# Top-k attention and SwiGLU on one Trainium2 core: units by query tile, FFN blocks across batches, and an issue order written out by hand

## The chip, the cores and the metric

The kernel runs on one core of one Trainium2 chip. The metric is the device time of an execution in microseconds (us). The engines are named as in the profile: PE is TensorE (PEld its weight loads), DVE is VectorE, ACT is ScalarE, POOL is GpSimd, and SP issues DMAs.

## The reference

There are 8 batches of 8 heads with 576 tokens and head dimension 64. For each head the scores are `q k^T / 8`; in each row only scores that are at least the row's 32nd largest are kept; softmax over those; product with `v`. The heads side by side give `x` of 4608 x 512. Then the feed-forward network (FFN):

```python
g = x @ w_gate                              # 512 x 1536
silu = g * (1.0 / (1.0 + np.exp(-g)))
val = x @ w_val                             # 512 x 1536
return (silu * val @ w_out).astype(np.float32)   # 1536 x 512
```

The weights arrive as float64. The kernel computes in float32.

## The kernel before

A pair of heads fills 128 partitions. The 576 tokens of a head are four tiles of 128 and a last one of 64. A unit of attention is (pair of heads, tile of queries), all five tiles of one pair before the next pair: 32 pairs, 160 units. In a full unit each head has its own tile of 128 queries; in the last unit of a pair the 64 queries of both heads share one.

The functions, with lines of the profile:
- `load` (L145) issues 12 DMAs for K, Q and V of a pair on SP (L152, L155). `prep` (L158) transposes K and Q on PE, copies them to SBUF on ACT, and puts V beside a column of ones on POOL (L184, L185).
- `scores` (L195): per head two products (512 and 64 keys) with contraction 64 (L206), then a copy to SBUF on ACT (L211).
- `select` (L214): four rounds of the eight largest (L227) with three of replacement between them (L237), on DVE. After the first, POOL makes the bias (L229) and ACT the exponentials (L231). At the end DVE multiplies the exponentials by the mask `s >= 32nd largest` (L240, two tensors read).
- `turn` (L250): ten transposes on PE (L260, L266) and three copies on ACT (L261, L267).
- `values` (L275): ten products in which the turned weights are the stationary operand and V with its ones (65 columns) the moving one (L287). The last column is the row's sum; DVE makes its reciprocal (L295, L296), ACT scales (L299), PE transposes to the layout of `x` transposed (L303), ACT copies (L306).
- `feed` (L316): the FFN of a batch in three blocks of 192 tokens. Twelve gate products (L326, four matmuls each) are copied to SBUF (L336), ACT takes a sigmoid of all at once (L338), POOL multiplies once over 2304 columns (L339), then twelve value products, each multiplied in from PSUM by DVE (L341), and the output products (L348), for a tile of 128 tokens and one of 64 with 512 columns each.
- `weights` and `rounded` (L127, L87): 72 pieces of 128 x 256 float64 weights are loaded by DMAs on POOL's queue (L91) and rounded on DVE, POOL and ACT.

A float32 matmul appears in the trace as two passes, and a transpose as one.

The order of the work comes from the loop at L368, which issues for each unit the next scores, its selection, the turn of the unit before, four pieces of FFN or weights, and the values of two units before; a scheduler then reorders instructions on every engine by their readiness as it estimates it. The FFN of a batch can start once the batch's attention is done. `ps_t` has two buffers for all transposes and value products.

Of the kernel before, what the change touches and what calls it, by code (L numbers as in the profile page):

```python
# [14 lines left out]
P = 128  # L15
TOP_K = 32
LOWEST = -3.4028234663852886e38
EPS = 1.0e-9
BLK = 192
WP = 256  # L20
HUGE = 122880.0  # 1151 << 20 as a float32's bits
LEAST = 3.4332275390625e-05  # 897 << 20 as a float32's bits
# [3 lines left out]
def kernel(  # L26
# [10 lines left out]
    """Top-k attention, then SwiGLU, in float32 throughout.  # L37

    Attention goes by unit (batch, pair of heads, tile of queries): the scores
    of both heads, the 32nd largest of each row by four rounds of max and three  # L40
    of match_replace, exp(s - max) zeroed below it, and the product with the
    values, whose last column of ones gives the sum of the row. A pair of heads
    is one 128-row slab of x transposed, which is what the first products of
    the FFN want. The FFN of a batch runs between the units of the next one.

    The tokens of a head are laid out as 4 tiles of the tokens 4 p + j, j < 4,
    and a last one of 64, so that each partition reads 1 KiB in one piece.

    The weights come in float64 and are rounded to float32 here, on their bits,
    while the first batch's attention runs.  # L50
    """
# [9 lines left out]
    DE = D + 1  # L61
    scale = 1.0 / float(D) ** 0.5
    assert D == 64 and R == 64 and H * D == DM and DM == 512 and S % BLK == 0

    consts = ctx.enter_context(tc.tile_pool(name="consts", bufs=1))
    ld = ctx.enter_context(tc.tile_pool(name="ld", bufs=2))
    work = ctx.enter_context(tc.tile_pool(name="work", bufs=2))
    small = ctx.enter_context(tc.tile_pool(name="small", bufs=4))
    conv = ctx.enter_context(tc.tile_pool(name="conv", bufs=2))
    ffn = ctx.enter_context(tc.tile_pool(name="ffn", bufs=2))  # L70
    ps_s = ctx.enter_context(tc.tile_pool(name="ps_s", bufs=2, space=PSUM))
    ps_t = ctx.enter_context(tc.tile_pool(name="ps_t", bufs=2, space=PSUM))
    ps_f = ctx.enter_context(tc.tile_pool(name="ps_f", bufs=2, space=PSUM))
# [3 lines left out]
    NV = 3  # L77
    vbufs = []
    for i in range(NV):
        vt = consts.tile([P, 2, J + 1, DE], FP32, name=f"v{i}")  # L80
        nc.gpsimd.memset(vt[:], 1.0)
        vbufs.append(vt)
# [4 lines left out]
    def rounded(src, dst):  # L87
# [36 lines left out]
            op0=ALU.is_ge, op1=ALU.mult,  # L124
        )

    def weights():  # L127
        pieces = []
        for src, dst in ((w_gate, wg), (w_val, wv), (w_out, wo)):
            for c in range(dst.shape[1]):  # L130
# [291 lines left out]
```

## Time and profile before

| what | value |
|---|---|
| median of three runs | 2607.87 us (2604.3, 2607.87, 2608.07) |
| span of the profiled execution, first to last instruction | 2599.7 us |
| median minus that span | 8.2 us |
| mean granted PE clock | 0.976 |
| busy 0 to 100 us: PE, DVE | 58, 79 us |
| busy 300 to 400 us: PE, DVE | 71, 94 us |
| busy 1100 to 1400 us: PE, DVE, ACT, POOL | 284, 236, 127, 25 us |
| busy 2430 to 2600 us: PE, DVE | 148, 12 us |
| matmul passes, DVE, ACT, POOL instructions | 12160, 4136, 2108, 473 |

The profiled execution's own time is that of its span; the runs' times include what lies before its first and after its last instruction. Engines work side by side, so their busy times are not to be added: at each stage the engine without idle time sets the pace, and idle time of the others costs nothing. A group line gives the line of the code, engine, operation, `out<-in`, shapes, count, then busy us, mean ns of one, idle us before it and what ended that wait. A timeline line gives the start, the time covered, and in brackets the idle time before it.

### The profile page before, as it was taken

To read this page: it belongs to the slowest core of one execution; us is meant where nothing else is said; L and a number is where in the kernel's file an instruction comes from. 1 tells how busy PE (TensorE), PEld (TensorE's weight loads), DVE (VectorE), ACT (ScalarE), POOL (GpSimd) and SP (SyncE) were. 2 spreads that over 40 slices of the span, in tenths; PEclk is the share of its full clock that TensorE was granted. 3 is DMA by queue.
4 is the path that set the end of the run, shared out by engine and by line. 5 is a ranking of instruction groups with operands and counts; after the bars stand their busy time and mean duration, and the time that the engine had idled before them with its cause. 6 is when DMAs were issued, how large, how long until landed. Compare 5 with 4: busy or idle time off the path is not lost. (4 is left out here: it accounts for less than half of the span.)

```text
span 2599.7 us, 33003 instructions
## 1 busy us (share of the span) xinstructions
PE 2325.9 (89%) x12160; PEld 1733.6 (67%) x12160; DVE 1911.0 (74%) x4136; ACT 971.4 (37%) x2108; POOL 314.3 (12%) x473
## 2 busy tenths in 40 slices
PE   5656579999999999999999999999999999999898
PEld 3444456667767668668667668668668667677666
DVE  7889898778787788769777788769768788765000
ACT  3333234335334335334434434434425434423111
POOL 3434321011011011011001001001101101000000
PEclk9999998999999999999999999999999999999999
DMA  3222110000000000000000000000000000000000
GB/s 100 61 67 71 62 34 14 21 17 19 21 19 17 20 7 19 16 21 15 21 20 15 21 16 19 7 20 15 21 20 15 21 16 1 7 7 5 7 5 11
DMA packets 128032, 58.75 MB, mean 23 GB/s; under 512 B 118656, under 2 KB 118656, under 8 KB 127872
## 3 DMA queue, kind: packets, MB, share of 16 engines
q1 hardware_dynamic: 122112, 37.78, 6.0%
q0 software_dynamic: 5760, 18.88, 2.4%
q8 instruction: 96, 1.57, 0.3%
q14 instruction: 64, 0.52, 0.1%
HBM read 47.19 MB, written 9.44 MB: 22 GB/s over the span
## 5 line engine op out<-in xcount | busy, mean ns | idle before, releaser
L227 DVE MAX8 m<-rest 128x8 f32<-128x576 f32 x864 | 619.8, 748 | 1.7
L326 PE MATMUL f<-xT,wv 128*128 128x192 f32 x2304 | 459.3, 349 | 76.1 <-DVE h L341 75.9
L348 PE MATMUL f<-wo,h 128*128 128x512 f32 (+1 forms) x1152 | 506.6, 595 | 0.0
L326 PEld LDWEIGHTS f<-xT,wv 128*128 128x128 f32 x2304 | 400.0, 203 | 99.0 <-DVE h L341 85.0
L287 PE MATMUL av<-v,et 128*128 128x65 f32 (+3 forms) x3200 | 455.4, 287 | 3.2 <-ACT et L261 3.0
L287 PEld LDWEIGHTS av<-v,et 128*128 128x128 f32 (+3 forms) x3200 | 417.4, 195 | 58.1 <-issue 14.1
L326 PE MATMUL f<-xT,wg 128*128 128x192 f32 x2304 | 419.6, 331 | 6.5 <-ACT g L336 6.5
L237 DVE MATCH_REPLACE8 rest<-m,rest 128x576 f32<-128x576 f32 x576 | 424.5, 742 | 0.0
L326 PEld LDWEIGHTS f<-xT,wg 128*128 128x128 f32 x2304 | 370.8, 191 | 22.1 <-ACT g L336 10.7
L348 PEld LDWEIGHTS f<-wo,h 128*128 128x128 f32 (+1 forms) x1152 | 183.0, 163 | 291.2 <-issue 288.1
L206 PE MATMUL s<-kT,qT 64*128 64x64 f32 (+3 forms) x1280 | 297.9, 483 | 84.3 <-ACT sc L211 84.1
L211 ACT COPY sc<-s 128x576 f32<-128x576 f32 x288 | 182.1, 642 | 438.1 <-PE s L206 323.4
L295 DVE TENSOR_SCALAR rinv<-av 128x2 f32<-128x2 f32 (+1 forms) x160 | 25.0, 156 | 358.2 <-PE av L287 351.2
L206 PEld LDWEIGHTS s<-kT,qT 64*128 64x128 f32 (+1 forms) x1280 | 154.2, 193 | 184.3 <-ACT sc L211 88.8
L231 ACT ACTIVATE e<-sc,bias 128x576 f32<-128x576 f32 x288 | 213.3, 771 | 166.8 <-POOL bias L229 166.3
L240 DVE SCALAR_TENSOR_TENSOR e<-sc,m,e 128x576 f32<-128x576 f32 x288 | 273.2, 981 | 2.0
L341 DVE TENSOR_TENSOR h<-h,f 128x192 f32<-128x192 f32 x288 | 96.9, 348 | 227.3 <-POOL h L339 134.6
L227 DVE MAX8 m<-sc 128x8 f32<-128x576 f32 x288 | 212.4, 749 | 35.3 <-ACT sc L211 33.9
L229 POOL TENSOR_SCALAR bias<-m 128x2 f32<-128x2 f32 (+1 forms) x160 | 34.8, 217 | 1480.2 <-DVE m L227 1344.1
L237 DVE MATCH_REPLACE8 rest<-m,sc 128x576 f32<-128x576 f32 x288 | 212.8, 742 | 0.0
L260 PE MATMUL main<-ident,e 128*128 128x128 f32 x1152 | 186.2, 302 | 14.5 <-DVE e L240 12.2
L356 ACT COPY o<-f 128x512 f32<-128x512 f32 (+1 forms) x48 | 28.0, 583 | 439.7 <-PE f L348 439.7
(52 smaller groups left out, 1565.9 us busy)
## 6 DMA issues: line engine op xcount, KB each, us to landing
k_in<-in_k_dram SPq DMA_DIRECT2D x64, 128.0 KB, 2.6
q_in<-in_q_dram SPq DMA_DIRECT2D x64, 128.0 KB, 2.6
v_in<-in_v_dram SPq DMA_DIRECT2D x64, 128.0 KB, 2.6
w<-in_moe_w_gate_dram POOLq DMA_DIRECT2D x24, 256.0 KB, 3.0
w<-in_moe_w_val_dram POOLq DMA_DIRECT2D x24, 256.0 KB, 3.0
w<-in_moe_w_out_dram POOLq DMA_DIRECT2D x24, 256.0 KB, 3.1
out_dram<-o SPq DMA_DIRECT2D x24, 256.0 KB, 2.2
out_dram<-o SPq DMA_DIRECT2D x24, 128.0 KB, 2.3
```

The lines of the kernel that those rows point to most:

```text
L206: nc.tensor.matmul(ps[x * R : x * R + ql, k0:k1], qT[d, qt * P : qt * P + ql], kT[d, k0:k1],)
L211: nc.scalar.copy(sc[:, t, :], ps[:, 0:S])
L227: nc.vector.max(m8[t], cur[t])
L229: nc.gpsimd.tensor_scalar_mul(bias[:, 0:nt], m[:, 0:nt, 0], -scale)
L231: nc.scalar.activation(e[:, t, :], sc[:, t, :], AF.Exp, bias=bias[:, t : t + 1], scale=scale)
L237: nc.vector.match_replace(rest[:], m8[t], cur[t], LOWEST)
L240: nc.vector.scalar_tensor_tensor(out=e[:, t, :], in0=sc[:, t, :], scalar=m[:, t, TOP_K - 1 : TOP_K], in1=e[:, t, :], op0=ALU.is_ge, op1=AL ...
L260: nc.tensor.transpose(main[:, cs], e[:, t, cs], ident[:])
L287: nc.tensor.matmul(av[0:ql, hh, :], et[0:kl, t, c, q0 : q0 + ql], vb[0:kl, hh, c, :], start=(c == 0), stop=(c == J),)
L326: nc.tensor.matmul(ps[:], w[:, c, m * P : (m + 1) * P], x[:, c, c0 : c0 + BLK], start=(c == 0), stop=(c == KC - 1),)
L341: nc.vector.tensor_mul(h[:, m, :], h[:, m, :], product(wv, m)[:])
L348: nc.tensor.matmul(ps[0:n, :], h[:, m, s0 - c0 : s0 - c0 + n], wo[:, m, :], start=(m == 0), stop=(m == MC - 1),)
```

## The change

Units now run by (batch, query tile, pair), so four pairs of K, Q and V are held at once and `x` becomes complete in tiles of tokens. The FFN runs in 18 blocks of 256 tokens that cross batch borders, and a block may start as soon as its columns of `x` are there. Its pieces are two gate products of 256 columns, two value products, or four output matmuls (18 pieces a block). The gate's SiLU is made per piece from tanh on ACT, with both multiplications on POOL; the value product is copied to SBUF by ACT first.

In `scores` the last 64 keys of both heads form one product with a block-diagonal stationary slab. In `select` DVE writes a penalty (-3e38 where the score is below the 32nd largest) from one tensor; in `weigh` POOL adds scores and penalty and ACT takes exponentials with their sums; `normalize` scales by the reciprocal sums on ACT before the turn. In `values` V is stationary and the turned weights move, which gives `x` transposed directly; the last 64 keys of both heads share one product with a block-diagonal V, for which two small DMAs are added.

The weights' DMAs are issued by SP, and eight weight pieces follow each unit. FFN pieces are issued by a credit of 2.3 per full unit and 1.15 per last unit, one ahead of `turn` and the others behind it. At the end every instruction on PE, DVE, ACT and POOL is tied to the one before it in the program, so each of these four engines keeps the order of issue; SP's order is still the scheduler's.

The diff, cut to its core:

```diff
-BLK = 192
+FAR = -3.0e38
+BLK = 256
...
+    slabs = ctx.enter_context(tc.tile_pool(name="slabs", bufs=5))
+    work = ctx.enter_context(tc.tile_pool(name="work", bufs=2))
+    small = ctx.enter_context(tc.tile_pool(name="small", bufs=3))
+    conv = ctx.enter_context(tc.tile_pool(name="conv", bufs=2))
+    ffn = ctx.enter_context(tc.tile_pool(name="ffn", bufs=2))
+    ps_s = ctx.enter_context(tc.tile_pool(name="ps_s", bufs=1, space=PSUM))
+    ps_t = ctx.enter_context(tc.tile_pool(name="ps_t", bufs=2, space=PSUM))
+    ps_f = ctx.enter_context(tc.tile_pool(name="ps_f", bufs=3, space=PSUM))
...
 def rounded(src, dst):
-        nc.gpsimd.dma_start(w[:], src.bitcast(I32).rearrange("p (f t) -> p f t", t=2))
+        nc.sync.dma_start(w[:], src.bitcast(I32).rearrange("p (f t) -> p f t", t=2))
...
+        for f in range(0, DFF, WP):
+            for src, dst in ((w_gate, wg), (w_val, wv)):
+                for c in range(KC):
+                    pieces.append((src[c * P : (c + 1) * P, f : f + WP], dst[:, c, f : f + WP]))
+        for c in range(MC):
+            for f in range(0, DM, WP):
+                pieces.append((w_out[c * P : (c + 1) * P, f : f + WP], wo[:, c, f : f + WP]))
...
+    def load(i):
+        b, hp = pairs[i]
+        kq = ld.tile([P, 2 * J + 1, 2, D], FP32, tag="kq", name="kq_in")
+        vt = slabs.tile([P, J + 1, 2, D], FP32, tag="v", name="v")
+        vl = vlast[i % NV]
+        for hh in range(2):
+            h = 2 * hp + hh
+            for n, src in ((0, k), (1, q)):
+                nc.sync.dma_start(
+                    kq[:, n * J : (n + 1) * J, hh, :],
+                    src[b, h, 0:JP].rearrange("(p j) d -> p j d", j=J),
+                )
+                nc.sync.dma_start(kq[n * R : (n + 1) * R, 2 * J, hh, :], src[b, h, JP:S])
+            nc.sync.dma_start(
+                vt[:, 0:J, hh, :], v[b, h, 0:JP].rearrange("(p j) d -> p j d", j=J)
+            )
+            nc.sync.dma_start(vt[0:R, J, hh, :], v[b, h, JP:S])
+            o = hh * R
+            nc.sync.dma_start(vl[o : o + R, o : o + R], v[b, h, JP:S])
+        raw[i] = (kq, vt, vl)
+    def prep(i):
+        kq, vt, vl = raw.pop(i)
+        slab = slabs.tile([P, JP + S], FP32, tag="kqT", name="kqT")
+        kl = klast[i % NV]
+        for c0, n, at in ((0, J, 0), (2 * J, 1, JP), (J, J, JP + R)):
+            ps = ps_t.tile([P, 512], FP32, tag="t", name="kqps")
+            for c in range(n):
+                nc.tensor.transpose(
+                    ps[:, c * P : (c + 1) * P],
+                    kq[:, c0 + c].rearrange("p h d -> p (h d)"),
+                    ident[:],
+                )
+            if n == 1:
+                nc.scalar.copy(slab[:, at : at + R], ps[:, R:P])
+                for o in (0, R):
+                    nc.scalar.copy(kl[o : o + R, o : o + R], ps[o : o + R, 0:R])
+            else:
+                nc.scalar.copy(slab[:, at : at + n * P], ps[:, 0 : n * P])
+        preps[i] = (slab, vt, vl, kl)
+    units = [(b, qt, hp) for b in range(B) for qt in range(J + 1) for hp in range(NHP)]
...
+    def scores(n):
+        b, qt, hp = units[n]
+        slab, _, _, kl = preps[b * NHP + hp]
+        ps = ps_s.tile([P, 3 * 512], FP32, tag="s", name="s")
+        sc = work.tile([P, 2 * S], FP32, tag="sc", name="sc", bufs=3)
+        halves = [slice(0, D), slice(D, P)]
+        if qt == J:
+            for hh, d in enumerate(halves):
+                nc.tensor.matmul(ps[d, 0:JP], slab[d, JP:S], slab[d, 0:JP])
+            for hh, d in enumerate(halves):
+                nc.tensor.matmul(ps[d, JP:S], slab[d, JP:S], kl[d, d])
+            nc.scalar.copy(sc[:, 0:S], ps[:, 0:S])
+        else:
+            qs = slice(S + qt * P, S + qt * P + P)
+            for hh, d in enumerate(halves):
+                nc.tensor.matmul(ps[:, 1024 * hh : 1024 * hh + JP], slab[d, qs], slab[d, 0:JP])
+            nc.tensor.matmul(ps[:, JP : JP + P], slab[:, qs], kl[:])
+            nc.scalar.copy(sc[:, 0 : JP + P], ps[:, 0 : JP + P])
+            nc.scalar.copy(sc[:, JP + P : 2 * S], ps[:, 1024:1536])
+        state[n] = dict(sc=sc)
+    def select(n):
+        nh = n_heads(units[n][1])
+        sc = state[n]["sc"]
+        m = small.tile([P, 2, TOP_K], FP32, tag="m", name="m")
+        heads = [slice(t * S, (t + 1) * S) for t in range(nh)]
+        rest = work.tile([P, 2 * S], FP32, tag="rest", name="rest", bufs=1)
+        e = work.tile([P, 2 * S], FP32, tag="e", name="e", bufs=3)
+        state[n] |= dict(m=m, e=e, heads=heads)
+        cur = sc
+        rounds = TOP_K // 8
+        for r in range(rounds):
+            if r == 2:
+                yield
+            for t, hs in enumerate(heads):
+                nc.vector.max(m[:, t, 8 * r : 8 * r + 8], cur[:, hs])
+            if r < rounds - 1:
+                for t, hs in enumerate(heads):
+                    nc.vector.match_replace(
+                        rest[:, hs], m[:, t, 8 * r : 8 * r + 8], cur[:, hs], LOWEST
+                    )
+                cur = rest
+        for t, hs in enumerate(heads):
+            nc.vector.tensor_scalar(
+                e[:, hs], sc[:, hs], m[:, t, TOP_K - 1 : TOP_K], FAR, ALU.is_lt, ALU.mult
+            )
+    def weigh(n):
+        st = state[n]
+        sc, m, e, heads = st.pop("sc"), st.pop("m"), st["e"], st["heads"]
+        nh = len(heads)
+        bias = small.tile([P, 2], FP32, tag="bias", name="bias")
+        nc.gpsimd.tensor_scalar_mul(bias[:, 0:nh], m[:, 0:nh, 0], -scale)
+        every = slice(0, nh * S)
+        nc.gpsimd.tensor_tensor(e[:, every], e[:, every], sc[:, every], ALU.add)
+        tot = small.tile([P, 2], FP32, tag="tot", name="tot")
+        for t, hs in enumerate(heads):
+            nc.scalar.activation(
+                e[:, hs], e[:, hs], AF.Exp, bias=bias[:, t : t + 1], scale=scale,
+                accum_out=tot[:, t : t + 1],
+            )
+        st["tot"] = tot
+    def normalize(n):
+        st = state[n]
+        tot, e, heads = st.pop("tot"), st["e"], st.pop("heads")
+        nh = len(heads)
+        nc.vector.tensor_scalar_add(tot[:, 0:nh], tot[:, 0:nh], EPS)
+        nc.vector.reciprocal(tot[:, 0:nh], tot[:, 0:nh])
+        for t, hs in enumerate(heads):
+            nc.scalar.mul(e[:, hs], e[:, hs], tot[:, t : t + 1])
+    def turn(n):
+        last = units[n][1] == J
+        e = state[n].pop("e")
+        et = work.tile([P, 2 * J + 1, P], FP32, tag="et", name="et")
+        for c0, cn in ((0, J), (J, 1)) if last else ((0, J), (J, 1), (J + 1, J)):
+            ps = ps_t.tile([P, 512], FP32, tag="t", name="etps")
+            kl = R if last and c0 == J else P
+            for c in range(cn):
+                k0 = (c0 + c) * P
+                nc.tensor.transpose(ps[0:kl, c * P : (c + 1) * P], e[:, k0 : k0 + kl], ident[:])
+            nc.scalar.copy(
+                et[0:kl, c0 : c0 + cn, :],
+                ps[0:kl, 0 : cn * P].rearrange("p (c j) -> p c j", c=cn),
+            )
+        state[n]["et"] = et
+    def values(n):
+        b, qt, hp = units[n]
+        _, vt, vl, _ = preps[b * NHP + hp]
+        et = state.pop(n)["et"]
+        last = qt == J
+        ql = R if last else P
+        av = ps_t.tile([P, P], FP32, tag="t", name="av")
+        if not last:
+            nc.tensor.matmul(av[:], vl[:], et[:, J, :], start=True, stop=False)
+        for c in range(J + 1 if last else J):
+            kl = R if c == J else P
+            for hh in range(2):
+                moving = (
+                    et[0:kl, c, hh * R : (hh + 1) * R]
+                    if last
+                    else et[:, c + hh * (J + 1), :]
+                )
+                nc.tensor.matmul(
+                    av[hh * R : (hh + 1) * R, 0:ql],
+                    vt[0:kl, c, hh, :],
+                    moving,
+                    start=last and c == 0,
+                    stop=c == (J if last else J - 1),
+                )
+        c0 = b * S + qt * P
+        at = c0
+        while at < c0 + ql:
+            kb = at // BLK
+            n_c = min((kb + 1) * BLK, c0 + ql) - at
+            if kb not in xT:
+                xT[kb] = ffn.tile([P, NHP, BLK], FP32, tag="xT", name="xT", bufs=3)
+                done[kb] = 0
+            nc.scalar.copy(
+                xT[kb][:, hp, at - kb * BLK : at - kb * BLK + n_c],
+                av[:, at - c0 : at - c0 + n_c],
+            )
+            done[kb] += n_c
+            at += n_c
...
+    def feed(kb):
+        x = xT.pop(kb)
+        hs = []
+        def product(w, s):
+            ps = ps_f.tile([P, 2, BLK], FP32, tag="f", name="f")
+            for i in range(2):
+                m = 2 * s + i
+                for c in range(KC):
+                    nc.tensor.matmul(
+                        ps[:, i, :],
+                        w[:, c, m * P : (m + 1) * P],
+                        x[:, c, :],
+                        start=(c == 0),
+                        stop=(c == KC - 1),
+                    )
+            return ps
+        for s in range(MS):
+            h = ffn.tile([P, 2, BLK], FP32, tag="h", name="h", bufs=MS + 1)
+            half = ffn.tile([P, 2, BLK], FP32, tag="gv", name="half_g", bufs=3)
+            ps = product(wg, s)
+            nc.scalar.activation(h[:], ps[:], AF.Tanh, scale=0.5)
+            nc.scalar.mul(half[:], ps[:], 0.5)
+            nc.scalar.add(h[:], h[:], 1.0)
+            nc.gpsimd.tensor_mul(h[:], h[:], half[:])
+            yield
+            val = ffn.tile([P, 2, BLK], FP32, tag="gv", name="val", bufs=3)
+            nc.scalar.copy(val[:], product(wv, s)[:])
+            nc.gpsimd.tensor_mul(h[:], h[:], val[:])
+            hs.append(h)
+            yield
+        for t in range(BLK // P):
+            ps = ps_f.tile([P, DM], FP32, tag="f", name="o_ps")
+            for m in range(MC):
+                nc.tensor.matmul(
+                    ps[:],
+                    hs[m // 2][:, m % 2, t * P : (t + 1) * P],
+                    wo[:, m, :],
+                    start=(m == 0),
+                    stop=(m == MC - 1),
+                )
+                if m % 4 == 3 and m < MC - 1:
+                    yield
+            o = ffn.tile([P, DM], FP32, tag="o", name="o")
+            nc.scalar.copy(o[:], ps[:])
+            store(o, kb * BLK + t * P)
+            yield
+    def piece():
+        while True:
+            if not current:
+                if not todo or done.get(todo[0], 0) < NHP * BLK:
+                    return False
+                current.append(feed(todo.pop(0)))
+            if next(current[0], 0) == 0:
+                current.pop()
+                continue
+            return True
+    def ahead(n):
+        b, qt, hp = units[n]
+        i = b * NHP + hp
+        if qt == 0:
+            prep(i)
+        if qt == J and i + NHP < len(pairs):
+            load(i + NHP)
+        scores(n)
+    for i in range(NHP):
+        load(i)
+    ahead(0)
+    credit = 0.0
+    for n in range(NU + 3):
+        if 0 <= n - 2 < NU:
+            values(n - 2)
+        if 0 <= n - 1 < NU:
+            weigh(n - 1)
+        if n + 1 < NU:
+            ahead(n + 1)
+        halves = select(n) if n < NU else iter(())
+        next(halves, None)
+        if n < NU:
+            credit = min(credit + (1.15 if units[n][1] == J else 2.3), 4.0)
+        for _ in range(4):
+            next(weight, None)
+        if credit >= 1 and piece():
+            credit -= 1
+        if 0 <= n - 1 < NU:
+            normalize(n - 1)
+        next(halves, None)
+        for _ in range(4):
+            next(weight, None)
+        if 0 <= n - 1 < NU:
+            turn(n - 1)
+        while credit >= 1 and piece():
+            credit -= 1
+    while piece():
+        pass
+    engines = {e.engine for e in (nc.tensor, nc.vector, nc.scalar, nc.gpsimd)}
+    before = {}
+    for ins in list(nc.cur_bb.bb.instructions):
+        if ins.engine in engines:
+            if ins.engine in before:
+                tc.add_manual_dep(
+                    ins,
+                    before[ins.engine],
+                    mybir.DependencyInfo(
+                        mybir.DependencyClass.NoSync, mybir.DependencyReason.DATA
+                    ),
+                    reason="order",
+                )
+            before[ins.engine] = ins.name
```

## The prediction

> **What bounds the kernel now.** I read the spans per core first (one core, span 2599.7 us, mean granted clock 0.976), then the page's busy shares and its 40 slices (65 us each):
>
> ```profile
> span 2599.7 us, 33003 instructions
> ...
> PE 2325.9 (89%) x12160; PEld 1733.6 (67%) x12160; DVE 1911.0 (74%) x4136; ACT 971.4 (37%) x2108; POOL 314.3 (12%) x473
> ...
> PE   5656579999999999999999999999999999999898
> ...
> DVE  7889898778787788769777788769768788765000
> ```
>
> There are three stages. Up to 400 us DVE sets the pace (79 to 94 of each 100 us, PE 58 to 71): weights are rounded and batch 0 has no FFN beside it. From 500 to 2430 us PE does (about 95%, DVE 78%). From 2430 us PE is alone with the last batch's FFN (DVE busy 12 of 170 us). Then the groups, for durations:
>
> ```profile
> L326 PE MATMUL f<-xT,wv 128*128 128x192 f32 x2304 | 459.3, 349 | 76.1 <-DVE h L341 75.9
> L231 ACT ACTIVATE e<-sc,bias 128x576 f32<-128x576 f32 x288 | 213.3, 771 | 166.8 <-POOL bias L229 166.3
> L211 ACT COPY sc<-s 128x576 f32<-128x576 f32 x288 | 182.1, 642 | 438.1 <-PE s L206 323.4 <-DVE e L240 88.9 <-DVE rinv L295 9.5
> L261 ACT COPY et<-main 128x512 f32<-128x512 f32 x288 | 163.5, 587 | 42.5 <-PE main L260 41.4
> L339 POOL TENSOR_TENSOR h<-h,g 128x2304 f32<-128x2304 f32 x24 | 122.8, 5117 | 293.3 <-ACT h L338 183.5 <-issue 55.4 <-PE f L326 54.4
> ```
>
> The reader is to see how small ACT and POOL are now: they can wait without cost. The last view is PE's timeline at two of its waits:
>
> ```profile
> 721.80 0.33 PE L287 MATMUL av<-v,et 128*128 128x65 f32 x2
> 726.09 5.49 PE L326 MATMUL f<-xT,wv 128*128 128x192 f32 x16 [3.95 <-DVE h L341]
> ```
> ```profile
> 1211.09 2.87 PE L326 MATMUL f<-xT,wv 128*128 128x192 f32 x16 [2.36 <-DVE h L341]
> ```
>
> The same 16 passes take 2.87 us after a wait of 2.36 us and 5.49 us after one of 3.95: PE falls to half speed when left idle. The granted clock does not show it: it reads 1.00 from 100 to 300 us, where a 512-column score pass takes 1.14 us against 0.63 later.
>
> **PE's work.** In the closing FFN a product of 8 passes of 192 columns recurs every 1.30 us, 0.1625 us a pass. By columns, 256 cost 0.217, and a new gate or value piece (16 passes) 3.47 us. The 48 output passes took 20.76 us, so an output piece of 8 costs 3.46. FFN before: 24 x (24 x 1.30 + 20.8) = 1248 us; after: 18 x 18 x 3.465 = 1123. Attention per full unit before: values 2.76, scores 1.23, ten transposes 1.2, x turned 0.2, sum 5.4. After: scores 1.1 (the 1.23 minus the 64-column passes, plus one 128-column product), nine transposes 1.06. V stationary is not in the trace: 18 passes of 128 columns cost 1.96 one after another (0.109 each by columns), or about 1.1 if the two heads' halves run side by side as the row halves of the scores do (eight passes, 2 us by columns, in 1.23). I take 1.3, nearer the scores. A unit falls to 3.5 us (3.3 to 4.1). So PE saves some 125 + 128 x 1.9 = 370 us, if it stays the bound.
>
> **DVE's work.** Two maxima in a row are 0.67 apart, load and replacement 0.73: 8 x 0.67 + 6 x 0.73 = 9.7. The penalty reads one tensor; between 0.37 (one-input L105, 0.20 apart at 256, by its slope) and 0.77 (today's masked product, two in 1.53). I take 0.37: its nearest row. With 0.35 for the sums, 10.9 us per full unit (up to 11.7), against 12.2 now with masked products and value products (L341, 97 us in all); 6.5 for a last unit, whose single head is a chain.
>
> **The fixed order is the point.** In steady state an iteration issues: PE values(n-2), scores(n+1), piece A, turn(n-1), piece or pieces B; ACT x, exp(n-1), scores' copies, A's outputs, e times 1/sum, turned copies, B's outputs; POOL bias and add(n-1), A's products, B's products. Each engine keeps it, so B's POOL product stands ahead of the add, the add ahead of exp, exp ahead of the copies, those ahead of A's outputs, those ahead of the normalization, and that ahead of turn on PE, with B behind it. With A a gate piece and B a value piece, from B's last pass on PE: copy to SBUF 0.2 + 0.59 = 0.8; POOL product of 512 (L339: 2.2 ns a column) 1.13 and hand-over 0.13, at 2.05; bias 0.2, add of 1152 columns 2.54, at 4.8; two exps 1.44, at 6.25; two copies 0.95 more, at 7.2; tanh, half, plus one 3 x 0.53 (512-column copies follow at 0.48, 576-column exps at 0.66), at 8.8; first head normalized 0.7, at 9.5; four transposes, their copy (two buffers in ps_t make the last four wait for it), four more, 1.8, at 11.3; B 3.47, at **14.8**. Neither PE (1.3 + 1.1 + 1.7 + 6.9 = 11.0) nor DVE (10.9) sets this. I take 14.9 (13.6, PE to ACT to PE alone, to 15.6, if a fixed part of POOL's time, some 0.27 by its 256-column row, adds to both).
>
> [...]
>
> **Sum.** Walking the credit rule: nine units without FFN; 119 full and 32 last units follow; 23 pieces are left over.
> - Start: SP issues one DMA per 0.65 us; the first 55 are K, Q, V, so weights land at 39 us instead of 6. First maximum at 15, first unit done at 65. Then eight units of 10.9 + 8 weight pieces x 2.6 (DVE 1.25, POOL add 0.8, DVE 0.42 in turn): 253. Sum 318 (2.4 to 3.0 a piece: 300 to 345).
> - 52 iterations with a gate or value piece and one B, 14.9: 775. 19 with two Bs, 18.4: 350. Seven with three, 20.7: 145. 27 with one output piece on either side, 11.4: 308; six with three, 14.9: 89. Eight with none or one, 11: 88. Sum 1755.
> - 28 preparations of K and Q: their copies stand behind exp on ACT and the scores behind them, 0.9 to 5.5 us each: 86.
> - 32 last units, A only: turned copy 0.7, values 1.6, scores 1.0, A 3.5, its outputs, one normalization, turn: 8 to 10, the six with a B 13: 312.
> - End: last unit's chain 6, 23 pieces 79, copy and store 6: 91.
>
> Total 318 + 1755 + 86 + 312 + 91 = 2562 us of span, against 2599.7. Matmul time was saved, and the chain has eaten it.
>
> To this the slow matmuls: in the 78 chain iterations PE is idle from A's end (5.9) to 9.6, and until B at 11.3 does only transposes. At 824 us even 2.58 idle after four transposes brought half speed (two passes in 1.01, otherwise 0.49). B then loses 2.7 us, as at 726. All of them: 78 x 2.7 = 211; last units 32 x 2.7 = 86. At 3.0 to 3.9 us the wait lies between the row that kept speed (2.88, at 457 us) and the one that did not, and transposes lengthen it; I take two thirds of 297, 198: span 2760. Median minus span is 8 today, which gives **2768 us**.
>
> [...]
>
> Costed at nothing: weight rounding's POOL and ACT steps (inside the 2.6), the 43 table loads that go (1.28 each, 55 us on ACT, which is busy 37%), the 72 weight DMAs that leave POOL's queue (0.58 each) for SP's, where only the start feels them, the 64 added V loads (0.65 each on SP, which is free for tens of us per batch), output stores. If SP held a store, ACT's copy would wait with all behind it.
>
> **Rivals.**
> 1. PE keeps its speed: the chain as above, 2570 us, **faster**. [...] Against: 726 and 824 us. It decides if fewer than 16 of the 110 slow starts happen (43 us).
> 2. The engines set the pace, the chain being hidden. Then 79 two-piece iterations x 11.0, 25 x 14.5, seven x 18, eight x 11: 1446; with preparations 42 (28 x 1.5), last units 245 (26 x 7, six x 10.5), start 318, end 91: 2142 + 8 = 2150 us. For: a unit's exp needs only its own add. Against: POOL's order puts B's product first.
> 3. Half speed also covers values, scores and A, which lengthens the chain itself: above 2900.
>
> **How the numbers follow.** Forecast 0.59 (2640 to 2900), rival 1 0.22 (2480 to 2610; 0.03 of it within 0.2%, about what a measurement of this kernel can tell), rival 2 0.12, rival 3 0.07. Faster 0.19 + 0.12 = 0.31, same 0.03, slower 0.66. The range takes forecast and rival 1: 2480 to 2900; the forecast's own is 2640 to 2900.
>
> **What would show it.** FFN iterations recur at 15 to 18 us, output-only ones at 11.4; PE waits for turn's e on ACT (L279), ACT's exp (L266) for POOL (L263), POOL for ACT's val (L382); DVE idles 4 us per unit at its sums (L276), busy under 70%; value products behind turn take over 5 us instead of 3.5. I am wrong if PE stays at 9 tenths, if DVE has no wait at L276, or if weights end far from 318 us.

## The result, and the profile after

The changed kernel takes 2814.73 us (median of four runs, 2813.23 to 2816.3), the kernel before 2607.42 beside it: 1.0806 times as long, 95% interval 1.0788 to 1.0824. The profiled execution's span is 2811.4 us, its mean granted clock 0.862.

The page of the changed kernel, cut to the lines that answer to those shown of before (40 slices, now of 70 us; the third row is the granted clock):

```profile
span 2811.4 us, 29146 instructions
PE 2057.6 (73%) x9888; PEld 1409.3 (50%) x9888; DVE 1719.7 (61%) x3848; ACT 1144.9 (41%) x2493; POOL 767.1 (27%) x696
PE   1222278687877888788878878688877888788889
DVE  3677756567655666567665756566754766576630
PEclk9755599798978998899889998888988998899889
```

No engine is the bound any more. PE has 2272 passes fewer and 268 us less busy time than before, and DVE 191 us less, but in the long middle PE is at 7 to 8 tenths where it was at 9, and DVE mostly at 5 to 7. The work fell and the time rose, so the engines wait for each other. The costliest groups of the changed kernel say who waits for whom (busy us, mean ns of one, idle us before, releaser):

```profile
L276 DVE TENSOR_SCALAR tot<-tot 128x2 f32<-128x2 f32 (+1 forms) x160 | 26.4, 165 | 849.3 <-ACT e L266 849.2
...
L263 POOL TENSOR_TENSOR e<-e,sc 128x1152 f32<-128x1152 f32 (+1 forms) x160 | 380.6, 2379 | 460.5 <-DVE e L251 307.8
L362 PE MATMUL f<-xT,wv 128*128 128x256 f32 x1728 | 470.0, 433 | 0.0
...
L362 PE MATMUL f<-xT,wg 128*128 128x256 f32 x1728 | 412.8, 394 | 0.0
...
L266 ACT ACTIVATE e<-e,bias 128x576 f32<-128x576 f32 x288 | 221.2, 771 | 259.0 <-POOL e L263 259.0
L383 POOL TENSOR_TENSOR h<-h,val 128x512 f32<-128x512 f32 x108 | 137.0, 1268 | 624.0 <-ACT val L382 624.0
```

DVE idles 849 us at its sums, for ACT's exponentials; ACT waits 259 us at those, for POOL's add; POOL waits 624 us at the FFN's value product, which in its fixed order stands ahead of that add. (The add's own wait for DVE, 308 us, lies mostly in iterations with output pieces, which give POOL no work; in the iteration below the add waits for nothing but POOL's own steps.) The two L362 rows do the same passes on the same shapes, yet a value pass takes 433 ns on average and a gate pass 394: value pieces mostly stand behind the turn, where PE has been idle.

One iteration with a gate piece ahead of the turn and a value piece behind it, in the timeline of the changed kernel (start, time covered, idle time before in brackets). Other engines' lines and DVE's are left out:

```profile
1506.98 0.38 PE L309 MATMUL av<-et,vlast 128*128 128x128 f32 x2
1507.18 0.59 ACT L382 COPY val<-f 128x512 f32<-128x512 f32 x1 [1.85 <-PE f L362]
...
1507.90 1.27 POOL L383 TENSOR_TENSOR h<-h,val 128x512 f32<-128x512 f32 x1 [1.24 <-ACT val L382]
...
1509.32 2.62 POOL L263 TENSOR_TENSOR e<-e,sc 128x1152 f32<-128x1152 f32 x1
...
1511.97 0.78 ACT L266 ACTIVATE e<-e,bias 128x576 f32<-128x576 f32 x1 [3.27 <-POOL e L263]
1512.65 0.19 ACT L266 ACTIVATION_READ_ACCUMULATOR e<-e,bias 128x1 f32 x1
...
1514.55 0.60 ACT L376 ACTIVATE h<-f 128x512 f32<-128x512 f32 x1
...
1516.04 1.45 ACT L279 ACTIVATE e<-e,tot 128x576 f32<-128x576 f32 x2
...
1516.92 1.09 PE L291 MATMUL etps<-ident,e 128*128 128x128 f32 x5 [3.60 <-issue]
...
1519.13 4.51 PE L362 MATMUL f<-xT,wv 128*128 128x256 f32 x16
...
1523.48 0.39 PE L309 MATMUL av<-et,vlast 128*128 128x128 f32 x2
```

This is the prediction's chain, link by link: piece B ends, its result is copied, multiplied on POOL, the add follows on POOL, the exponentials, the two score copies and A's three outputs follow on ACT, then the normalization, the turn, and the next B. It closes after 1523.48 - 1506.98 = 16.5 us. B itself takes 4.35 us (to the next iteration's first product) where a piece at full speed takes 3.46 (e3, 1516.77 to 1520.23).

The granted clock of this iteration says why, when it is read in short windows (start and end, length, busy us and instructions of PE, PEld, DVE, ACT and POOL, then the granted clock, share and GB/s of DMA):

```profile
1506.98:1517.50 10.52, 6.92 (x45) 4.94 (x43) 3.84 (x10) 6.37 (x13) 5.30 (x4) 1.00 0.00 0
1517.55:1520.90 3.35, 3.14 (x11) 2.49 (x11) 3.35 (x7) 1.34 (x3) 0.00 (x0) 0.50 0.00 0
1520.95:1523.48 2.53, 2.53 (x13) 2.22 (x12) 2.53 (x7) 0.00 (x0) 0.00 (x0) 1.00 0.00 0
```

The clock is halved for 3.4 us, from the transposes to the middle of B, and for no longer.

By stages (PE's busy time in each): until the first FFN piece 344 us (72), from there to the last unit 2370 us (1898), the end 97 us (87).

### The profile page after: what moved, and what is told of

It reads as the page before. It is cut to its first block, busy times and chain, and to the rows that moved or that the text cites. A ratio compares the mean times of both kernels' runs of the same rounds, so it can differ in the third digit from the quotient of the medians.

```text
span 2811.4 us, 29146 instructions
## 1 busy us (share of the span) xinstructions
PE 2057.6 (73%) x9888; PEld 1409.3 (50%) x9888; DVE 1719.7 (61%) x3848; ACT 1144.9 (41%) x2493; POOL 767.1 (27%) x696
## 4 chain that ended last, share of the span: by engine, by line
PE 67%; issue 12%; ACT 9%; DVE 7%; POOL 4%; SPq 1%; DMA 0%; POOLq 0%; ACTq 0%; DVEq 0%
PE f L362 29%; PE o_ps L389 14%; PE etps L291 8%; PE av L318 6%; PE s L222 5%; ACT et L292 3%; PE s L223 2%; POOL e L263 2%; POOL bits L130 2%; ACT e L266 2%; DVE m L243 1%; PE kqps L187 1%; PE s L215 1%; DVE rest L246 1%; ACT kqT L197 1%
## 5 line engine op out<-in xcount | busy, mean ns | idle before, releaser
L291 PE MATMUL etps<-ident,e 128*128 128x128 f32 (+1 forms) x1312 | 270.2, 337 | 584.3 <-issue 353.8
L276 DVE TENSOR_SCALAR tot<-tot 128x2 f32<-128x2 f32 (+1 forms) x160 | 26.4, 165 | 849.3 <-ACT e L266 849.2
L291 PEld LDWEIGHTS etps<-ident,e 128*128 128x128 f32 (+1 forms) x1312 | 175.7, 165 | 700.3 <-issue 434.9
L263 POOL TENSOR_TENSOR e<-e,sc 128x1152 f32<-128x1152 f32 (+1 forms) x160 | 380.6, 2379 | 460.5 <-DVE e L251 307.8
L362 PE MATMUL f<-xT,wv 128*128 128x256 f32 x1728 | 470.0, 433 | 0.0
L362 PEld LDWEIGHTS f<-xT,wv 128*128 128x128 f32 x1728 | 382.5, 227 | 63.5
L362 PE MATMUL f<-xT,wg 128*128 128x256 f32 x1728 | 412.8, 394 | 0.0
L389 PE MATMUL o_ps<-wo,h 128*128 128x512 f32 x864 | 405.4, 617 | 0.0
L362 PEld LDWEIGHTS f<-xT,wg 128*128 128x128 f32 x1728 | 337.8, 200 | 47.6 <-issue 0.5
L266 ACT ACTIVATE e<-e,bias 128x576 f32<-128x576 f32 x288 | 221.2, 771 | 259.0 <-POOL e L263 259.0
L383 POOL TENSOR_TENSOR h<-h,val 128x512 f32<-128x512 f32 x108 | 137.0, 1268 | 624.0 <-ACT val L382 624.0
L292 ACT COPY et<-etps 128x512 f32<-128x512 f32 (+1 forms) x448 | 195.0, 472 | 196.8 <-PE etps L291 189.6
L279 ACT ACTIVATE e<-e,tot 128x576 f32<-128x576 f32 x288 | 210.0, 778 | 23.4 <-DVE tot L277 23.4
L318 PE MATMUL av<-et,v 128*64 128x128 f32 (+2 forms) x2688 | 202.2, 293 | 10.5 <-ACT et L292 10.5
L382 ACT COPY val<-f 128x512 f32<-128x512 f32 x108 | 63.3, 586 | 317.3 <-PE f L362 317.3
L222 PE MATMUL s<-kqT 64*128 64x512 f32 x512 | 176.3, 771 | 21.6 <-ACT kqT L197 21.6
```

The costliest lines, as they stand in the source:

```text
L222: nc.tensor.matmul(ps[:, 1024 * hh : 1024 * hh + JP], slab[d, qs], slab[d, 0:JP])
L263: nc.gpsimd.tensor_tensor(e[:, every], e[:, every], sc[:, every], ALU.add)
L266: nc.scalar.activation(e[:, hs], e[:, hs], AF.Exp, bias=bias[:, t : t + 1], scale=scale, accum_out=tot[:, t : t + 1],)
L279: nc.scalar.mul(e[:, hs], e[:, hs], tot[:, t : t + 1])
L291: nc.tensor.transpose(ps[0:kl, c * P : (c + 1) * P], e[:, k0 : k0 + kl], ident[:])
L292: nc.scalar.copy(et[0:kl, c0 : c0 + cn, :], ps[0:kl, 0 : cn * P].rearrange("p (c j) -> p c j", c=cn),)
```

## The experiments

**Theory:** the order in which the engines are made to issue closes a ring through POOL, ACT and PE, longer than any engine's work; half speed of PE after the waits adds to it. **Rivals:** PE's half speed is the main loss; POOL is too slow for the add, wherever it stands; the new work itself (V stationary, tanh, the crossing blocks) costs more than it saves, in any order. All times below are medians, with the ratio to the kernel before run beside them (2604.2 to 2607.0 us).

**e1_add_early**: bias and add move from `weigh`, behind the last B's POOL product, to right behind the unit's own selection, one iteration earlier in POOL's order.

```diff
-    def weigh(n):
+    def penalize(n):
...
         nc.gpsimd.tensor_tensor(e[:, every], e[:, every], sc[:, every], ALU.add)
+        st["bias"] = bias
+
+    def weigh(n):
+        e, heads, bias = st["e"], st["heads"], st.pop("bias")
...
         next(halves, None)
+        if n < NU:
+            penalize(n)
```

> One edit: POOL's bias and add of a unit are issued right behind that unit's selection, ahead of the FFN pieces behind turn, instead of at the start of the next iteration. Theory (the fixed order chains B's POOL product, add, exp, scores' copies, A's outputs, normalization and turn): the product of B (1.3 us) and the add (2.6) leave the chain; what remains is values 1.3, scores 1.4, A 3.5, A's outputs 0.8 to 1.8, normalization 0.7, turn 2.2, B 3.5 to 4.4, about 14.3 us per FFN iteration in place of 16.7, over some 78 iterations: 2815 - 185 = about 2630 us, and DVE's wait for the sums falls by about 2 us per iteration. Rival (PE's half speed or the lower granted clock alone make the difference, and the order is harmless): within 30 us of 2815.

Measured: 2670.6 us, 1.0239 (1.0219 to 1.0259), 144 us less than the changed kernel. The gate-and-value iteration falls from a mean of 16.7 us to 15.5 (30 iterations that hold no preparation of K and Q). Eight of the 30 take 14.0 us, as the chain would have it; in them the clock is never halved. The other 22 take 15.1 to 17.0, with a stretch of 3.41 or 6.83 us at half clock, though PE waits the same 2.4 us in all 30. That is one reason why the edit gains less than expected; the other is that the start got longer (370 us instead of 344): there the add now stands ahead of the second four weight pieces on POOL.

**e2_out_late**: ACT's and POOL's steps on piece A's result are issued behind the turn's copies instead of ahead of the normalization.

```diff
             ps = product(wg, s)
+            yield 2
             nc.scalar.activation(h[:], ps[:], AF.Tanh, scale=0.5)
...
-        if credit >= 1 and piece():
+        if credit >= 1 and piece(True):
             credit -= 1
...
             turn(n - 1)
+        outputs()
```

> One edit: the ACT and POOL steps on the results of the piece ahead of turn (tanh, half, plus one, products; or copy and product; or output copy) are issued behind turn's copies instead of ahead of the normalization. PE's order is the same. Theory (chain): A's outputs, 0.6 to 1.6 us, leave the chain in full and last units: 78 x about 1.3 plus 26 x 1.1 and less waiting afterwards, 2815 - 130 to 220 = 2595 to 2685 us; exp still waits for POOL's add. Rival (half speed alone): within 30 us of 2815.

Measured: 2592.27 us, 0.9939 (0.9919 to 0.9959), 222 us less than the changed kernel. The gate-and-value iteration has a mean of 14.3 us (11.4 to 16.7).

**e3_both**: both edits together.

> Both edits: the add early, A's outputs behind turn. Theory (chain): nothing but PE's own work and DVE's is left, 11.3 us per iteration with two pieces in place of 16.7, 15 with three, preparations about 2 us in place of 7, last units 8 in place of 10 to 13; start 344 and end 91 as they are: 344 + 1500 + 60 + 255 + 91 = about 2250 us, faster than the kernel before. PE then has no long wait, so gate and value passes run at one speed (wv mean as wg). Rival (half speed alone, or the engines' work itself): over 2600 us.

Measured: 2298.17 us, 0.8816 (0.8802 to 0.8831), 517 us less than the changed kernel with the same arithmetic, and 48 more than expected, of which 26 are the longer start of e1. Its PE slices (57 us each), its two FFN rows, and PE's timeline:

```profile
PE   2112126989899899989998999899988999899999
```
```profile
L366 PE MATMUL f<-xT,wg 128*128 128x256 f32 x1728 | 396.9, 383 | 0.0
L366 PE MATMUL f<-xT,wv 128*128 128x256 f32 x1728 | 396.2, 383 | 0.0
```
```profile
1515.00 0.71 PE L295 MATMUL etps<-ident,e 128*128 128x128 f32 x5
1516.28 0.66 PE L295 MATMUL etps<-ident,e 128*128 128x128 f32 x4 [0.57 <-ACT et L296]
1516.77 3.62 PE L366 MATMUL f<-xT,wg 128*128 128x256 f32 x16
1520.23 0.38 PE L313 MATMUL av<-et,vlast 128*128 128x128 f32 x2
...
1522.95 3.62 PE L366 MATMUL f<-xT,wv 128*128 128x256 f32 x16
1526.41 0.71 PE L295 MATMUL etps<-ident,e 128*128 128x128 f32 x5
```

The iteration is 1526.41 - 1515.00 = 11.4 us, and PE's only idle time in it is 0.57 us: PE is the bound again, as the prediction's rival 2 had it. Gate and value passes now cost the same 383 ns, since the halved clock is gone from these iterations: of the 44 that have a gate or value piece ahead of the turn, one piece behind it and no preparation, 43 have a stretch of it in the changed kernel and none here. The two edits give more together than apart: 1.1 and 2.3 us of the gate-and-value iteration alone, 5.3 together, and 144 and 222 us of the kernel alone, 517 together. Part of that is the clock: behind the start it is halved 112 times in the changed kernel, 83 in e1, 66 in e2 and 19 here, with a mean granted clock of 0.862, 0.880, 0.883 and 0.928.

**e4_warm**: nothing of the order changes, but PE multiplies on while it waits for the turn: four products (two ahead of a last unit) whose result the transposes overwrite, wherever piece A is a gate or value piece.

```diff
+            for _ in range(filled):
+                nc.tensor.matmul(ps[:], wg[:, 0, 0:P], wg[:, 1, 0:512])
+            filled = 0
             for c in range(cn):
```

> One edit: where the piece ahead of turn is a gate or value product, PE is given four idle-time matmuls of 512 columns (two in front of a last unit's turn) into the buffer of the first transposes, just ahead of turn; 3.5 us of work in a wait of 3.6 us. They change no output. Theory: they cost nothing of themselves and keep PE at full speed, so B takes 3.5 us in place of 4.4 and the transposes run faster: about 1.2 us in each of 78 iterations and some in last units, 2815 - 95 to 130 = 2685 to 2720 us, with the chain left as it is. Rival (granted clock falls with PE's load, or the wait is no wait): the added 8 passes of 0.43 us lengthen each iteration, 2815 + 100 or more.

Measured: 2682.14 us, 1.0283 (1.0263 to 1.0304), 133 us less than the changed kernel although PE does 700 passes more. PE's timeline of this kernel:

```profile
1485.51 3.60 PE L290 MATMUL etps<-wg 128*128 128x512 f32 x8
1489.33 0.90 PE L295 MATMUL etps<-ident,e 128*128 128x128 f32 x5 [0.22 <-ACT e L279]
1490.63 0.66 PE L295 MATMUL etps<-ident,e 128*128 128x128 f32 x4 [0.41 <-ACT et L296]
1491.12 3.62 PE L366 MATMUL f<-xT,wv 128*128 128x256 f32 x16
```

The filling ends ahead of the wait's own end (0.22 us remain), so it holds nothing up; transposes and B then run at full speed, and the iteration is 15.2 us in place of 16.7. None of the 44 iterations counted under e3 has a halved clock any more. Half speed at these waits therefore costs some 133 us. Elsewhere it remains, most of it around the preparations of K and Q: PE is busy for 144 us at half clock behind the start. At full speed that would give back at most half, 72 us (an estimate), and 2682 - 72 = 2610 us. So the first rival falls: without any half speed the kernel would still be no faster than the one before.

**e6_dve_add**: the changed kernel with its add on DVE, in two halves.

```diff
-        nc.gpsimd.tensor_tensor(e[:, every], e[:, every], sc[:, every], ALU.add)
+        for hs in heads:
+            nc.vector.tensor_tensor(e[:, hs], e[:, hs], sc[:, hs], ALU.add)
```

> The changed kernel with one edit: scores plus penalty are added on DVE (two instructions of 576 columns) in place of POOL (one of 1152, 2.62 us). Theory (chain): B's POOL product and the add both leave the way from B to exp, as with the early add, and the add itself shortens by about 1 us; DVE's 10.9 us per unit becomes 12.5 and stays under the chain: 2600 to 2680 us in place of 2815. Rival (DVE's time is what counts): 128 x 1.6 us longer, 3000 us.

Measured: 2676.42 us, 1.0278 (1.025 to 1.0305): 138 us less, about as much as e1 gives by order alone (144). PE's wait at the turn is now named as ACT's; in the changed kernel only 82 us of it were, and most was listed as below. The first line is of the changed kernel's waits, the second of e6's:

```profile
PE etps L291 <- issue: 353.8, 92, 14.8
```
```profile
PE etps L292 <- ACT e L280: 362.4, 126, 16.2
```

**e7_both_dve_add**: the same edit on e3, where the add is off the ring.

> The kernel with both orders mended (2298 us), with the same edit: the add on DVE in place of POOL. Theory: here nothing waits in a chain, DVE's 11 us stand beside PE's 11.3 us, and 1.6 us more make DVE the bound: 128 x about 1.3 plus 32 x 0.8: 2298 + 150 to 200 = about 2470 us. So the same move gains in the chained order and loses in the other. Rival (a shorter way to exp counts in any order): under 2298 us.

Measured: 2311.58 us, 0.8877 (0.8851 to 0.8902), only 13 us more than e3. As the add has left POOL, the start is shorter (the FFN begins at 352 us instead of 370), so from there on e7 is some 32 us longer. The expectation was still a miss: it let DVE's work in a full unit (12.1 us with the add, above PE's 11.4) set every iteration. DVE is busy 190 us more than in e3 (1906.2 against 1716.1), and its wait at the sums shrinks from 327 to 188 us. 139 us of the added work went into time in which DVE had waited. Two-piece iterations stay at 11.4 us, and the longer ones (three pieces, about 15 us, or a preparation, 13 to 21 us) let DVE catch up. POOL is thus not the wrong place for the add as such: in e3 nothing is gained by taking it away from there, in the changed kernel 138 us are, by where it stands.

**e5_start**: e3 with the start mended: the first two weight DMAs behind the first pair's loads, pairs 3 and 4 loaded one iteration later each, and the add behind the second weight pieces for the first nine units.

```diff
-    for i in range(NHP):
-        load(i)
+    load(0)
+    next(weight)
+    load(1)
     ahead(0)
...
+        if n < 2:
+            load(n + 2)
...
-        if n < NU:
+        if 9 <= n < NU:
             penalize(n)
...
+        if n < min(9, NU):
+            penalize(n)
```

> The kernel with both orders mended (2298 us), with its start mended too: the first two weight DMAs go out behind the first pair's K, Q and V, the third and fourth pair's loads one iteration later each, and in the first nine iterations POOL's add is issued behind the second four weight pieces (issued ahead of them it made those iterations 36.8 us in place of 33.4). Theory (the start is a chain of SP issues and then of DVE and POOL in turn): the first iteration falls from 52 to about 35 us and eight others by 3.4: 2298 - 17 - 27 = about 2254 us. Rival (weights are not what the start waits for): 2298 - 27 or less change.

Measured: 2258.56 us, 0.8672 (0.8653 to 0.869). The FFN begins at 330 us instead of 370; all of the gain is there.

**e8_scheduler**: the changed kernel without the block that ties each instruction to the one before it; a scheduler orders it, as it does the kernel before.

```diff
-            if ins.engine in before:
-                tc.add_manual_dep(
...
```

> The changed kernel without the instructions tied to one another: every engine's order is the scheduler's, by its estimate of readiness; all the rest of the change stays. Theory (the fixed order costs what the chain adds): at least 150 us faster than 2815, since a ready add, exp or turn may pass pieces that are not ready. Rival (the change's other parts cost the time: more ACT and POOL steps, half speed): within 50 us of 2815 or above.

Measured: 2201.7 us, 0.8455 (0.8433 to 0.8477): 613 us less than the changed kernel. Its page (slices of 55 us) and two lines of POOL's timeline:

```profile
PE 1882.0 (85%) x9888; PEld 1289.2 (59%) x9888; DVE 1754.0 (80%) x3848; ACT 1135.9 (52%) x2493; POOL 779.8 (35%) x696
...
PE   5333787899989899999998989888998898998999
```
```profile
1507.85 2.62 POOL L263 TENSOR_TENSOR e<-e,sc 128x1152 f32<-128x1152 f32 x1 [1.18 <-DVE e L251]
...
1514.77 1.27 POOL L379 TENSOR_TENSOR h<-h,half_g 128x512 f32<-128x512 f32 x1 [1.00 <-ACT h L378]
```

The add starts when DVE's penalty is there, with no FFN product ahead of it. The third rival falls with this run: the same arithmetic is 15% faster than the kernel before.

**e9_mended_scheduler**: e5 without that block.

> The kernel with both orders and the start mended (2259 us), without the instructions tied: the scheduler's order from the mended order of issue. Theory: both it and the untied changed kernel (2202 us) are held by PE in the steady state (92 and 91 of 100 us busy) and differ by the first 350 us, where the scheduler starts FFN work sooner; the order of issue then matters little to it: 2170 to 2215 us. Rival (the mended order of issue also helps the scheduler where it gained on the tied kernel, 2815 to 2298): under 2150 us.

Measured: 2183.69 us, 0.8381 (0.8367 to 0.8395), the fastest of all. Against e5 the difference lies in the start: from 400 to 2100 us PE is busy 1557 us in e5 and 1558 in e9, from 0 to 400 us 140 and 232 (in e8 1552 and 232). Of these 92 us, 75 reach the end. Mended by hand, the order equals the scheduler's once the FFN runs; it loses where weights, loads and attention begin.

**e10_before_tied**: the reverse, the kernel before with that same block added.

> The kernel before with one edit: every instruction on PE, DVE, ACT and POOL tied to the one before it in the program, as the changed kernel has it. Theory (a fixed order of issue makes engines wait for one another): value products then wait on DVE for a whole selection, and DVE in turn for the last two of four products and for the values, some 2 us more per full unit on average: 2607 + 128 x 1.5 to 2.5 = 2800 to 2930 us. Rival (tying costs nothing, what cost the time is this change's order alone): within 50 us of 2607.

Measured: 3332.61 us, 1.2791 (1.2766 to 1.2817). The direction held, the size was far under. Two waits of it, and after them the same two of the kernel before untied:

```profile
DVE rinv L295 <- PE av L287: 809.5, 127, 24.7
...
PE xps L303 <- ACT x L299: 386.4, 160, 15.4
```
```profile
DVE rinv L295 <- PE av L287: 351.2, 124, 22.3
...
PE xps L303 <- ACT x L299: 61.7, 61, 2.7
```

The kernel before lived by its scheduler: as issued, its value products stand behind four FFN products, DVE waits there for the sums, and PE then waits for x. How the 728 us divide among such waits was not taken further.

**Where the time went.** With the scheduler's order on both sides, the change's parts are worth 2607 - 2202 = 406 us, and the fixed order takes 613. Of these 613, 517 come back with two moved steps (e3) and 40 with the mended start (e5). The last 57 lie ahead of 400 us, as far as the busy times of e8 and e5 tell: e8 begins its FFN at 142 us, e5 at 330.

## Why the prediction was right

**The sign and the size.** 2768 us was predicted, 2814.7 measured, 1.7% more and inside the range. The span was missed by 51 us (2760, 2811); the 8 us added to it were 3 in the changed kernel. The mechanism is shown: each link stands in the timeline, and moving two of its links, without touching the arithmetic, gives 517 us (e1, e2, e3).

**PE's work.** V stationary was taken at 1.3 us; 1.34 measured (0.31 + 1.03, by starts in e3), scores 1.4 by starts instead of 1.1, and an FFN piece 3.46. PE's saving was there, as e8 shows, and the order kept it from counting.

**The chain.** 14.9 us taken, 15.2 at full speed (e4). Missed in it: two accumulator reads of 0.19 us behind the exponentials, and the turn, from the first transpose to B, 2.2 us instead of 1.8 in the changed kernel (1.8 in e4, so this belongs to half speed).

**The slow matmuls.** The term was 198 us; e4 gives 133. The place was right, the count and the price were both wrong, in opposite directions. The count: two thirds of the slow starts were taken, but a halved clock appears in 76 of the 77 full-unit iterations with a gate or value piece ahead of the turn and in 21 of the 23 of last units. The price: 2.7 us, read at 726 us, against 1.5 in a two-piece iteration (16.7 against 15.2). The clock gives the reason. At 726 us of the kernel before it was halved for 6.8 us, over the whole piece:

```profile
725.30:732.10 6.80, 6.01 (x20) 6.02 (x21) 4.63 (x13) 1.44 (x2) 0.21 (x1) 0.50 0.00 0
```

In 34 of the 44 two-piece iterations of the changed kernel (those with a gate or value piece ahead of the turn and no preparation) it was halved for 3.41 us, which at half speed can cost 1.7 us at most (an estimate: half of it). Of the loss 0.4 us fell on the turn and 1.2 on B, on average. Split by unit, the loss is 107 us in full units (141 predicted) and 24 in last units (57).

The prediction says that the granted clock does not show the half speed. This line shows it. What was read as 1.00, from 100 to 300 us, was no reading: in this trace the clock's record begins at 370 us, and the view counts the time ahead of it as 1.00, so that the mean of 0.976 says nothing of the start. Nor does the length of the wait alone decide: the prediction set 2.88 us, which kept the speed, against 3.95, which did not, but in e1 the same wait of 2.4 us kept it in eight iterations and lost it in 22. What decides there was not tried, and that transposes lengthen a wait, as the prediction has it from one place (824 us), no run shows.

**The rest of the sum** was too short by what e4 shows, where the chain's waits no longer slow PE: 2681 us of span against 2562 without slow matmuls, 119 us. In the prediction's own terms, the largest error is the preparations of K and Q: beside iterations with the same pieces and none, the 28 cost 152 us in e4 (142 in the changed kernel) instead of 86, up to 10 us each instead of 5.5. Their wait was foreseen (5.4 us for ACT's copy at 520 us of e4), but not the half speed behind it: there four score passes take 2.08 us instead of 1.13, and A 5.14 instead of 3.62. The start, up to the iteration with the first FFN piece, is 341 us instead of 318 (a weight piece 2.85 us, not 2.6), the other time of full units 1772 instead of 1755, of last units 322 instead of 312, the end 94 instead of 91. So the 2768 rests on errors of opposite sign: 65 too much in the slow matmuls, 119 too little elsewhere, 54 in all, of the 51 by which the span was missed. That it came so near is in part luck.

**Rivals.** Rival 1's mechanism was tried by e4, and 2682 instead of 2570 came out: it would not have been faster than before. Its deciding point (16 of 110 slow starts) was wrong by the 119 us above: even with none the kernel would not have won. Rival 2 did not occur, but e3 makes it real by order alone: two-piece iterations of 11.4 us (11.0 taken), three-piece of 14.8 (14.5), 2298 us against 2150, of which the preparations (110 us against 42) and the start (366 against 318) are the most. Rival 3 did not occur in the chain: score products and A ran at full speed there (A 3.62 us at 1509.70). Behind the preparations it did, as told above, and the whole stayed under 2900.

**What would show it.** FFN iterations of 15 to 18 us: 16.7 came. Output-only 11.4: 11.4 in most. DVE busy under 70%: 61%, its idle time at the sums 849 / 160 = 5.3 us a unit instead of 4. The waits named at L266, L383 (for L382) and L276 are there; that at L291 is mostly listed under "issue". Weights ended at 342 us instead of 318. Value pieces behind the turn over 5 us: 4.1 to 5.0 came, 4.6 on average, the one sign that failed, with the price of half speed.

## What to carry to other kernels

When every engine keeps a hand-written order, follow one iteration round from the last step of a piece to its next start through all queues: if the ring is longer than the busiest engine's work, steps that others wait for are issued too late, and moving them can be worth more than the work that a change saves (here POOL's add and ACT's outputs gave 517 us, the change's parts 406). Judge such a change by its parts and its order apart; a run without the ties says which of the two it is. Size an engine's slack by the mean iteration and not by the most frequent one, as e7 shows.

## What the runs showed of the hardware

- In the changed kernel each exponential with a running sum is followed by a read of the accumulator on ACT of 0.19 us (L266, 288 of them), two in each full unit.
- In e4 four products that nobody reads, put into PE's wait, made the kernel 133 us faster, with a mean granted clock of 0.926 instead of 0.862. In the trace of the changed kernel the clock takes two values, 1.00 and 0.50, and from 344 to 2714 us the lower stands in 112 stretches: 69 of 3.41 us, 34 of 6.83 and nine of 10.24. The length of a wait alone did not tell whether one follows: behind 2.4 us one did in 22 iterations of e1 and did not in eight.
- The mean granted clock covers only what was recorded: in the profiled execution of the kernel before the record begins at 370 us, and from 100 to 300 us the column reads 1.00 while a score pass of 512 columns takes 1.05 to 1.22 us, against 0.59 to 0.69 from 1100 to 1400 us.
- Two column halves of PE ran side by side: in the changed kernel the value passes of the two heads (64 columns of the stationary operand each, the first at 1523.80 us) start in pairs, 0.006 to 0.008 us apart, from the second on with a pair every 0.109 us. In e3 the 16 passes of 128 columns take 1.03 us (1520.54 to 1521.57), 0.064 each, where 128 columns would cost about 0.108 one after another (an estimate: half of the FFN's 0.216 for 256, 3.46 / 16).
- A long wait was listed under "issue" although an engine ended it: 353.8 us at the turn of the changed kernel. In the timeline above ACT's two normalizations begin at 1516.04, 0.7 us each, and the transposes start at 1516.92, behind the first; in e6 the wait at the same place is named as ACT's, 362.4 us.
